# A hand-written order for a recurrent attention and token mixer: every operation re-ordered, other PSUM banks, and 196 more transposed blocks in two 64-row halves

## The chip, the cores and the metric

The program runs on one core of a Trainium2 chip. A core has a matrix engine (PE, whose weight loads the profile lists apart as PEld), a vector engine (DVE), an activation engine (ACT), a general engine (POOL) and a queue that issues transfers (SP). Each engine runs its own list of instructions strictly in order and waits at an instruction until the semaphores that it needs have been raised. Matmuls write to PSUM, which has 8 banks of 512 float32 per partition; all other data are in SBUF.

The metric is device time in microseconds (us), as the median of three runs: 199.9 us before the change (199.68 to 200.76).

## The reference

Two stages, for batch B = 4, H = 8 heads, S = 768 tokens, D = 40. The first is a recurrence over the tokens, with a 40 x 40 state for each batch and head. The second mixes the output over tokens and channels.

```python
for t in range(S):
    y[t]  = r[t] @ state                                   # per batch and head
    Sa    = state @ a[t]
    state = state * w[t] - outer(Sa, b[t]) + outer(v[t], k[t])
x = y as (B, S, 320)
theta  = x @ w_theta
zr, zi = x * cos(theta), x * sin(theta)
u      = x + w_tok_r @ zr + w_tok_i @ zi                   # over the tokens
out    = u + relu(u @ w_ch)
```

## The kernel before

The recurrence is done in chunks of 128 tokens: 6 chunks for each batch, 24 in all, numbered i = 0 to 23. For a chunk the kernel loads w, k, b, a, v and r (160 KB each, in rows of 160 bytes) and does the following.

- `prep(i)`: ln w on ACT, running sums as matmuls (`cs`, `cx`), exponentials on ACT (`exp`, `ew`), products that scale k, b and a (`kb`, two of them, and `ah`, mostly on POOL, line 456), and casts of v and r. Then the scaled k and b (`tkb`, 8 blocks), a (`ta`, 4), v (`tv`, or `to` and `tb` in chunks 0 to 7) and r (`tr`, 8) are transposed in blocks of 128 x 128 on PE. Copies on ACT or DVE bring the result from PSUM to SBUF (`ekb`, `ea`, ...).
- `attention_scores(i)` and `readout(i)`: four 128 x 128 score matrices per head (`spsi`, `sphi`, `slv`, `slu`, line 603). They are matmuls over 64 rows. Each is masked as it leaves PSUM (`mpsi`, `mphi`, `mlv`, `mlu`): on DVE in one multiply (line 612), or on ACT with a second pass on POOL (lines 614 and 616).
- `recurrence(i)`: the serial part. `x0` needs the state of the chunk before, then come `nx`, `nu`, `enu`, the new state (`gt`, `egt`, `wgt`) and its transpose (`gd`, `egd`).
- `y` and `ex` give x for the chunk. `theta(i)` transposes x (`xt`) and multiplies by w_theta (`th`). `sines` takes cos and sin on ACT, and `z` multiplies them with x, on POOL (line 894) or on DVE (line 893).
- `mix_row`: for each of the 24 output blocks, 12 matmuls over the tokens (`row`, line 910), a sum on DVE (`uadd`, line 916), a transpose (`ut`), the channel matmul (`ch`), and the result (`oo`) and its store. They need all z of their batch, so the rows of one batch run among the chunks of the next, and those of the last batch at the end.
- The mixer's weights: `wdma` issues 18 transfers on POOL's queue (lines 961 and 989): w_theta and w_ch in 6 pieces of 160 or 40 KB, and 12 blocks of rows of the two token matrices at 192 KB each. `wt` transposes the token matrices on PE.

Nothing is scheduled at run time. The kernel records 1602 operations, and `order()` then emits them by three tables. `ORDER` is one list over all operations; an engine gets its own operations in the sequence in which they stand there. `HOMES` gives each PSUM tile its bank. `PICK` names operations that take their other form: a copy on the other engine, a mask on ACT and POOL instead of DVE, a product on the other engine, or a transpose in halves.

```python
def order(self):
    for n, m in PICK.items():
        o = self.ops[n]
        o.eng, o.fn = o.alts[m - 1][:2]
        if o.eng == "PE":
            o.new = (o.new[0], 2)          # a transpose in halves takes two banks
    out = [self.ops[n] for n in ORDER]
```

A transpose has two forms (`turned`, lines 404 and 408; `turn_runs`, lines 569 and 572 for r and the early v). The whole form is one matmul per block: 128 rows against a 128 x 128 identity. The form in halves is two matmuls per block, rows 0 to 63 and rows 64 to 127, each against a 64 x 64 identity, with the results in two neighbouring banks.

Loads go through SP's queue in the sequence of `ORDER`. Each raw buffer has 2 to 5 copies, so a load waits until the product that read that buffer before is done, and every load behind it waits too. 11 transposes are done by the transfer engines (`CROSSBAR`), the same 11 in both kernels.

## Time and profile before

| what | value |
|---|---|
| timed runs | 199.9 us median, 199.68 to 200.76 |
| profiled execution, first to last instruction | 195.9 us; no other time is given for that execution, so 4.0 us of the median lie outside its span |
| instructions in it | 8473, 3516 of them matmuls |
| PE, DVE, ACT, POOL busy | 184.3, 163.3, 150.6, 145.1 us |
| read from memory, written | 29.54 MB, 3.93 MB |
| granted clock of PE | 0.997 on average |

A row of the page's fifth part names line, engine, operation, output and inputs, then the count, busy time, mean duration in ns, and the idle time ahead of it with what ended that. In the timeline, neighbours of one kind are merged: start, length, engine, line, operation and count. Matmuls overlap, so what one costs PE is read from the distance between starts and not from its length.

### The profile page before, as it was taken

What the parts mean: (1) busy time and instruction counts of PE and PEld (TensorE: products, weight loads), DVE (VectorE), ACT (ScalarE), POOL (GpSimd) and SP (SyncE); (2) the same over time, 40 slices, a digit from 0 to 9 for tenths busy, and PEclk for the clock granted to TensorE, in tenths of its full rate; (3) what the DMA queues carried; (4) which work ended last, traced back from release to release, by engine and by line L of the source; (5) the groups of instructions that cost most, each with busy time, mean ns of one, the idle gap of its engine ahead of it and who ended that gap; (6) DMA issues with size and microseconds to landing.
All of it is one profiled execution on the core that took longest, in us unless ns stands there. A gap on an engine that the chain in (4) does not pass through costs nothing.

```text
span 195.9 us, 8473 instructions
## 1 busy us (share of the span) xinstructions
PE 184.3 (94%) x3516; PEld 145.4 (74%) x3516; DVE 163.3 (83%) x260; ACT 150.6 (77%) x336; POOL 145.1 (74%) x211
## 2 busy tenths in 40 slices
PE   7889899999997999999899999999999999999992
PEld 6767687887786778887577787887788768767661
DVE  5378799999998999898897999999999938664453
ACT  3575879799997997999689599979999867575111
POOL 8367466579969999696699959868879997469100
PEclk9999999999999999999999999999999999999998
DMA  5999897999999999979999997789899977535055
GB/s 118 217 205 182 148 214 157 174 171 206 216 183 166 197 180 185 225 122 200 179 183 158 166 200 129 164 147 180 161 178 203 168 172 102 128 136 74 32 197 172
DMA packets 134646, 32.78 MB, mean 167 GB/s; under 512 B 124816, under 2 KB 134608, under 8 KB 134608
## 3 DMA queue, kind: packets, MB, share of 16 engines
q1 hardware_dynamic: 131680, 29.19, 76.6%
q0 software_dynamic: 2784, 2.97, 9.3%
q8 instruction: 27, 0.44, 0.9%
q10 hardware_dynamic: 144, 0.08, 0.1%
q14 instruction: 11, 0.09, 0.1%
HBM read 29.54 MB, written 3.93 MB: 171 GB/s over the span
## 4 chain that ended last, share of the span: by engine, by line
PE 61%; DMA 12%; POOL 9%; ACT 6%; DVE 4%; SPq 4%; issue 2%; ACTq 0%; DVEq 0%; POOLq 0%
PE banks L910 16%; PE banks L603 9%; PE banks L404 8%; PE banks L792 5%; DMA raw_a<-in_a_dram 4%; DMA raw_kb<-in_k_dram 4%; SPq L436 3%; PE banks L408 3%; DMA uT<-up 2%; PE banks L569 2%; PE banks L663 2%; POOL kb L456 2%; PE banks L686 2%; PE banks L802 2%; DMA raw_v<-in_v_dram 2%
## 5 line engine op out<-in xcount | busy, mean ns | idle before, releaser
L456 POOL TENSOR_TENSOR kb<-raw_kb,ex 128x320 bf16<-128x320 f32 x46 | 37.1, 814 | 8.0 <-DMA raw_kb<-in_k_dram 3.0
L910 PE MATMUL banks<-zr,wtok_r 128*128 128x320 bf16 x144 | 41.0, 300 | 0.2
L910 PE MATMUL banks<-zi,wtok_i 128*128 128x320 bf16 x144 | 40.8, 299 | 0.1
L456 POOL TENSOR_TENSOR ah<-raw_a,we 128x320 bf16<-128x320 f32 x22 | 19.0, 865 | 12.9 <-ACT we L506 4.7
L612 DVE TENSOR_TENSOR lamu<-banks,mask_p 128x1024 bf16<-128x1024 f32 x22 | 26.8, 1219 | 1.5 <-PE banks L603 0.8
L612 DVE TENSOR_TENSOR psi<-banks,mask_p 128x1024 bf16<-128x1024 f32 x22 | 26.8, 1219 | 0.8 <-PE banks L603 0.7
L612 DVE TENSOR_TENSOR phi<-banks,mask_n 128x1024 bf16<-128x1024 f32 x18 | 21.9, 1216 | 1.6 <-POOL r L462 1.3
L612 DVE TENSOR_TENSOR lamv<-banks,mask_p 128x1024 bf16<-128x1024 f32 x17 | 20.7, 1219 | 1.6 <-PE banks L603 1.0
L894 POOL TENSOR_TENSOR zi<-cs,xp 128x320 bf16<-128x320 f32 x22 | 17.2, 791 | 2.0 <-ACT cs L879 1.2
L910 PEld LDWEIGHTS <-wtok_r 128*128 128x128 bf16 x144 | 14.0, 97 | 5.6 <-issue 0.3
L603 PE MATMUL banks<-aT,kbT 64*128 64x128 bf16 x384 | 17.2, 217 | 0.9 <-DVE kbT L426 0.3
L894 POOL TENSOR_TENSOR zr<-cs,xp 128x320 bf16<-128x320 f32 x22 | 17.4, 802 | 0.1
L910 PEld LDWEIGHTS <-wtok_i 128*128 128x128 bf16 x144 | 14.0, 98 | 3.8 <-issue 0.3
L829 PE MATMUL banks<-kb,lamv 128*128 128x40 bf16 x192 | 14.9, 180 | 0.0
L831 PE MATMUL banks<-kb,lamu 128*128 128x40 bf16 x192 | 14.8, 179 | 0.0
L603 PEld LDWEIGHTS <-kbT 64*128 64x128 bf16 x384 | 11.8, 94 | 3.7 <-ACT kbT L422 1.1
L829 PEld LDWEIGHTS <-lamv 128*128 128x128 bf16 x192 | 13.2, 96 | 0.4
L916 DVE TENSOR_TENSOR up<-banks,xp 128x320 bf16<-128x320 f32 x22 | 10.6, 485 | 3.1 <-PE banks L910 2.9
L831 PEld LDWEIGHTS <-lamu 128*128 128x128 bf16 x192 | 13.0, 96 | 0.0
L472 ACT ACTIVATE lw<-raw_w 128x320 bf16<-128x320 f32 x24 | 11.5, 477 | 1.5 <-DMA raw_w<-in_w_dram 1.3
L496 ACT ACTIVATE ex<-banks 128x328 f32<-128x328 f32 (+1 forms) x24 | 10.8, 450 | 2.2 <-PE banks L491 1.1
L822 PE MATMUL banks<-gd,rT 128*128 128x80 bf16 x80 | 12.2, 197 | 0.0
(202 smaller groups left out, 583.0 us busy)
## 6 DMA issues: line engine op xcount, KB each, us to landing
raw_w<-in_w_dram SPq DMA_DIRECT2D x24, 160.0 KB, 4.3
raw_v<-in_v_dram SPq DMA_DIRECT2D x24, 160.0 KB, 3.7
raw_a<-in_a_dram SPq DMA_DIRECT2D x24, 160.0 KB, 3.9
raw_kb<-in_k_dram SPq DMA_DIRECT2D x24, 160.0 KB, 4.2
raw_kb<-in_b_dram SPq DMA_DIRECT2D x24, 160.0 KB, 4.2
raw_r<-in_r_dram SPq DMA_DIRECT2D x24, 160.0 KB, 3.8
out_dram<-oo SPq DMA_DIRECT2D x9, 160.0 KB, 2.6
wrow_i<-in_moe_w_tok_i_dram POOLq DMA_DIRECT2D x6, 192.0 KB, 5.3
```

Of the source, the lines that this page charges most:

```text
L404: nc.tensor.transpose(out=t[:, m * 128:m * 128 + 128], in_=src, identity=ident)
L456: pool = ("POOL", lambda: nc.gpsimd.tensor_tensor(out=dst, in0=in0, in1=in1, op=ALU.mult))
L472: add("ACT", "ln", i, lambda: nc.scalar.activation(out=paired(lw)[:, :, :, 0:D], in_=paired(raw_w[s4]), func=AF.Ln), 473, [("raw_w", s4)], ...
L496: got = add("ACT", "exp", i, lambda: nc.scalar.activation(out=ex[:, :, 0:D] if no_total else ex.rearrange("p h x -> p (h x)"), in_=sums(ps ...
L603: nc.tensor.matmul(t[:, q, g, :], lhsT=lhs[g][rows(q)], rhs=rhs[g][rows(q)], start=True, stop=True)
L612: add("DVE", kindm, i, lambda: nc.vector.tensor_tensor(out=flat, in0=whole(), in1=mask.to_broadcast([128, 2 * G, 128]), op=ALU.mult), 1217 ...
L822: nc.tensor.matmul(t[:, g * 80:g * 80 + 80], lhsT=by_two(rT)[g], rhs=gd[:, 2 * g:2 * g + 2, :], start=True, stop=False, skip_group_check=True)
L829: nc.tensor.matmul(o, lhsT=lamv[:, p, g, :], rhs=kb[:, 0, h, 0:D], start=first, stop=False, skip_group_check=True)
L831: nc.tensor.matmul(o, lhsT=lamu[:, p, g, :], rhs=kb[:, 1, h, 0:D], start=False, stop=True, skip_group_check=True)
L894: pool = ("POOL", lambda: nc.gpsimd.tensor_tensor(out=dst, in0=in0, in1=in1, op=ALU.mult))
L910: nc.tensor.matmul(acc(), lhsT=wtok[nm][j][:, s], rhs=zs[c][:, s], start=n == 0 and c == 0, stop=n == NT - 1 and c == 1)
L916: add("DVE", "uadd", q, lambda: nc.vector.tensor_tensor(out=u, in0=acc(), in1=x, op=ALU.add), 488, [pk, x_key(q)], [u_key(q)], at="row")
```

## The change

All three tables are new, and so is `WARM`, which only names other banks for its 49 warming matmuls. The computation is the same 1602 operations.

- `ORDER`: another sequence on every engine, loads and weight transfers included.
- `HOMES`: other banks for the PSUM tiles.
- `PICK`: 164 entries in place of 135. Transposes in halves grow by 196 blocks net (`tkb` from 8 chunks to 18, `nut` from 2 to 8, `ut` from 1 to 7, `tr` from 6 to 9, `xt` from 5 to 7, `tv` from 5 to 7, `ta` from 7 to 8, `to` and `tb` from 0 to 2 each). Copies, masks and products change engine too: 7 products `z` are on DVE instead of 2, 4 of the products `kb` instead of 2, and 4 copies `ekb` instead of 7.

```diff
-    0, 7, 3, 6, 1, 20, 2, 21, 8, 23, 24, 4, 27, 32, 9, 30, 22, 33, 31, 25, 5, 34, 26, 12, 28,
+    0, 6, 20, 21, 22, 23, 24, 3, 7, 32, 33, 35, 27, 30, 34, 36, 37, 38, 2, 26, 1, 25, 28, 31, 8,
...
-    25: 1, 31: 1, 37: 1, 39: 1, 40: 1, 48: 1, 49: 1, 75: 1, 80: 1, 85: 1, 86: 1, 115: 1, 118: 1,
+    28: 1, 29: 1, 31: 1, 33: 1, 34: 1, 36: 1, 38: 1, 40: 1, 48: 1, 49: 1, 60: 1, 64: 1, 74: 1,
...
-WARM = {21: (0, 25), 30: (1, 4), 33: (2, 1), 28: (1, 8), 41: (1, 11)}
+WARM = {21: (3, 25), 33: (3, 1), 30: (2, 4), 28: (5, 8), 41: (6, 11)}
```

The new file is two lines longer ahead of the functions, so its line numbers are larger by 2: line 410 of the new kernel is line 408 of the old.

Three places show how the instructions move.

First, POOL at the start of the program, after its last memset. `wth`, `wch` and `wrow` are the mixer's weights; `kb` and `ah` are products, and `r` and `o` casts of r and v. Before:

```order
L334 MEMSET wth 64x320
L456 TENSOR_TENSOR kb_128<-raw_kb_73,ex_174 128x8x40
L462 CAST r_136<-raw_r_80 128x16x40
L616 AFFINE_SELECT phi_200<-phi_200 128x1024
L961 DMA wth<-in_moe_w_theta_dram 64x320
L961 DMA wth<-in_moe_w_theta_dram 128x2x320
L456 TENSOR_TENSOR kb_129<-raw_kb_74,ex_175 128x8x40
```

And now:

```order
L336 MEMSET wth 64x320
L963 DMA wth<-in_moe_w_theta_dram 128x2x320
L963 DMA wch<-in_moe_w_ch_dram 64x320 x2
L963 DMA wth<-in_moe_w_theta_dram 64x320
L963 DMA wch<-in_moe_w_ch_dram 128x2x320
L991 DMA wrow_r_247<-in_moe_w_tok_r_dram 128x768
L991 DMA wrow_i_249<-in_moe_w_tok_i_dram 128x768
L991 DMA wrow_i_248<-in_moe_w_tok_i_dram 128x768
L464 CAST r_136<-raw_r_80 128x16x40
L618 AFFINE_SELECT phi_200<-phi_200 128x1024
L458 TENSOR_TENSOR ah_126<-raw_a_69,we_179 128x8x40
L458 TENSOR_TENSOR kb_129<-raw_kb_74,ex_175 128x8x40
```

Eight weight transfers, 1016 KB, now stand ahead of the cast of r. Before, two of them (200 KB) stood behind the first `kb`, cast and select. The product `kb_128` of chunk 0 has gone to DVE.

Second, DVE at the start, after its memsets. `psi` and `lamv` are masked scores, `aT`, `kbT` and `vT` copies of transposes, and `v` a copy of v turned back. Before:

```order
L455 TENSOR_TENSOR ah_125<-raw_a_68,we_178 128x8x40
L422 COPY aT_184<-banks 128x512
L455 TENSOR_TENSOR kb_128<-raw_kb_73,ex_174 128x8x40
L422 COPY v_132<-banks 128x512
L612 TENSOR_TENSOR psi_198<-banks,mask_p 128x1024
L422 COPY v_133<-banks 128x512
L455 TENSOR_TENSOR ah_126<-raw_a_69,we_179 128x8x40
L455 TENSOR_TENSOR kb_129<-raw_kb_74,ex_175 128x8x40
L612 TENSOR_TENSOR lamv_202<-banks,mask_p 128x1024
```

And now:

```order
L457 TENSOR_TENSOR ah_125<-raw_a_68,we_178 128x8x40
L426 COPY vT_193<-banks 128x512
L457 TENSOR_TENSOR kb_128<-raw_kb_73,ex_174 128x8x40 x2
L424 COPY aT_184<-banks 128x512
L428 COPY kbT_187<-banks 128x2x8x64
L614 TENSOR_TENSOR psi_198<-banks,mask_p 128x1024
L457 TENSOR_TENSOR kb_129<-raw_kb_74,ex_175 128x8x40
L981 CAST wth<-banks 64x320
L981 CAST wth<-banks 128x320
L614 TENSOR_TENSOR lamv_202<-banks,mask_p 128x1024
```

Both products of chunk 0 and its copy of the transposed k and b are on DVE ahead of the first mask, and two copies of w_theta stand between the first mask and the second.

Third, PE at the transpose of k and b of chunk 1 (`kb_129`); `wide` holds the identity. Before:

```order
L603 LDWEIGHTS nuT_196
L603 MATMUL banks<-rT_190,nuT_196 128x128
L404 LDWEIGHTS kb_129
L404 MATMUL banks<-wide,kb_129 128x128
...
L569 LDWEIGHTS o_139
L569 MATMUL banks<-wide,o_139 128x32x4
```

And now:

```order
L406 LDWEIGHTS ah_126
L406 MATMUL banks<-wide,ah_126 128x128
L410 LDWEIGHTS kb_129
L410 MATMUL banks<-wide,kb_129 128x64
...
L715 LDWEIGHTS gt_142
L715 MATMUL banks<-wide,gt_142 128x80
```

Eight matmuls of 128 columns have become sixteen of 64 columns, and they now stand between two groups of 128-row matmuls instead of after a group of 64-row ones.

242 rows, old and new, of tables (HOMES, ORDER, PICK) are left out of this document.

## The prediction

> **What bounds the kernel now.** I read the page's slices first, then busy time by stage, the waits of PE, the chain of waits, and the timeline of POOL's transfers.
>
> ```profile
> PE   7889899999997999999899999999999999999992
> DVE  5378799999998999898897999999999938664453
> DMA  5999897999999999979999997789899977535055
> ```
>
> Three resources run at nine tenths for most of the span: PE to the end, DVE to about 155 us, the transfer engines from 5 us to about 110. So the first question is which of them paces which stage.
>
> ```profile
> 10.00:20.00 10.00, 8.57 (x167) 6.90 (x167) 8.49 (x12) 6.43 (x17) 7.17 (x9) 1.00 1.02 196
> 20.00:60.00 40.00, 37.76 (x774) 30.73 (x771) 37.79 (x47) 35.42 (x88) 28.27 (x38) 1.00 0.96 183
> 60.00:100.00 40.00, 38.83 (x852) 30.70 (x853) 36.79 (x54) 35.58 (x76) 34.75 (x50) 1.00 1.02 179
> 100.00:150.00 50.00, 49.75 (x1112) 39.94 (x1111) 47.53 (x74) 45.03 (x106) 43.02 (x58) 1.00 0.92 171
> 175.00:190.00 15.00, 15.00 (x137) 10.62 (x136) 7.73 (x17) 4.43 (x11) 7.10 (x10) 1.00 0.32 78
> ```
>
> The columns are length, then busy time of PE, weight loads, DVE, ACT and POOL, then granted clock, transfer share and GB/s. From 10 to 100 us the transfers are full (0.96 to 1.02) and DVE is at 92 to 95% from 20 us on. From 100 us PE is hardly idle (49.75 of 50, then 15.00 of 15) at a full clock. So work taken from PE pays surely only late in the program. Early, it pays as far as loads and DVE let the chunks come sooner.
>
> ```profile
> PE banks L408 <- POOL ah L456: 1.2, 2, 0.9
> 48.22 7.07 DMA raw_kb<-in_k_dram
> 86.11 8.33 DMA raw_a<-in_a_dram
> raw_a<-in_a_dram SPq DMA_DIRECT2D x24, 160.0 KB, 3.9
> 45.09 0.60 POOL L989 DMA_DIRECT2D wrow_i<-in_moe_w_tok_i_dram  x1
> 85.67 1.14 POOL L989 DMA_DIRECT2D wrow_i<-in_moe_w_tok_i_dram  x2
> 86.79 1.08 POOL L989 DMA_DIRECT2D wrow_r<-in_moe_w_tok_r_dram  x2
> ```
>
> PE's longest wait is for a product on POOL. The chain of waits has two loads of 7 to 8 us, where the median of such a load of a is 3.9. Both stand among `wrow` transfers of POOL's queue. The one at 86.11 us was issued amid four of them, 768 KB between 85.67 and 87.87 us. Such a group thus makes a load up to 8.33 - 3.9 = 4.4 us later.
>
> **What a half block saves.**
>
> ```profile
> 30.30 0.61 PE L569 MATMUL banks<-wide,o 128*128 128x128 bf16 x8
> 30.74 0.28 PE L404 MATMUL banks<-wide,xp 128*128 128x128 bf16 x2
> 127.59 0.41 PE L408 MATMUL banks<-wide,kb 64*128 64x64 bf16 x16
> 127.93 0.31 PE L910 MATMUL banks<-zr,wtok_r 128*128 128x320 bf16 x1
> 133.43 0.39 PE L404 MATMUL banks<-wide,nu 128*128 128x128 bf16 x4
> 133.75 0.29 PE L408 MATMUL banks<-wide,ah 64*128 64x64 bf16 x8
> 133.88 0.40 PE L408 MATMUL banks<-wide,kb 64*128 64x64 bf16 x16
> 134.11 0.22 PE L603 MATMUL banks<-rT,vT 64*128 64x128 bf16 x2
> 180.44 3.26 PE banks L910 x24
> ```
>
> From start to start, eight whole blocks take 0.44 us, 55 ns each. Sixteen halves, eight blocks, take 0.23 us when 64-row work follows and 0.34 when 128-row work follows. Four whole blocks ahead of 64-row work take 0.32 us, where four at 55 ns make 0.22. So a block in halves costs 28 ns, a saving of 27, and a change between 64-row and 128-row work costs 0.09 to 0.10 us in either direction. The last row gives 0.136 us for a `row` matmul.
>
> The new order halves 196 more blocks, 5.3 to 5.5 us. I counted the changes between the two kinds of matmul in the order of PE's instructions: 156 before, 174 now. The 18 more cost 1.6 us. PE's whole gain is 3.8 us, whatever the rest does.
>
> **Where it falls.** I cut the order at two marks that both kernels have: `x0` of chunk 21, and `y` of chunk 23, the last attention work. In the trace before they stand here, the first with its first matmul, the second with its last:
>
> ```profile
> 156.23 0.20 PE L644 MATMUL banks<-gt,aT 128*128 128x80 bf16 x1
> 176.02 0.18 PE L831 MATMUL banks<-kb,lamu 128*128 128x40 bf16 x1
> ```
>
> *To x0(21).* 162 of the blocks: -4.5 us. 14 of the changes: +1.3. Two more parts of `row`, each of two matmuls at 0.136: +0.5. PE: -2.7 us. DVE also loses work here, by these rows:
>
> ```profile
> L612 DVE TENSOR_TENSOR phi<-banks,mask_n 128x1024 bf16<-128x1024 f32 x18 | 21.9, 1216 | 1.6 <-POOL r L462 1.3
> L422 DVE COPY aT<-banks 128x512 bf16<-128x512 bf16 x5 | 2.1, 418 | 0.7 <-PE banks L404 0.7
> L422 DVE COPY kbT<-banks 128x1024 bf16<-128x1024 bf16 x3 | 2.1, 688 | 0.3 <-ACT gd L718 0.3
> L455 DVE TENSOR_TENSOR kb<-raw_kb,ex 128x320 bf16<-128x320 f32 x2 | 1.7, 870 | 1.1 <-DMA raw_kb<-in_b_dram 1.1
> ```
>
> Two masks fewer (-2.4), three copies `kbT` fewer (-2.1), net four small copies fewer at 0.42 (-1.7), two products `kb` more (+1.7), and the rest, one to three short operations of each kind (`ewo`, `ewt`, `eth`, `enu`, `ext`, `ah`), nets to +1.0. Sum: -3.5 us. ACT gains about 1.7 us and POOL 1.9 to this mark. Both were at 90% or less, so I cost that at nothing. If ACT had no room left, it would be its 1.7 us. As PE and DVE both fall, I take the smaller of the two: **-2.7**, with 0 (the loads pace the chunks) and -3.5 as bounds.
>
> *From x0(21) to y(23).* 12 blocks (-0.3), one part of `row` (-0.3), two `ch` and their 64-row pair (-0.7), and one `xt` (-0.2) fewer: **-1.4**. PE is the only full engine here, so I take it in full; the bounds are -1.4 and 0.
>
> *After y(23).* Those two `ch` come back (+0.7), one part of `row` fewer (-0.3), 22 blocks in halves (-0.6), the moved `xt` and two changes (+0.3): **+0.1** for PE. But three of the last eight products `z` of chunk 21 go to DVE, while POOL does the others.
>
> ```profile
> 178.77 1.11 DVE L893 TENSOR_TENSOR zi<-cs,xs 128x320 bf16<-128x320 f32 x1
> 178.74 0.79 POOL L894 TENSOR_TENSOR zi<-cs,xp 128x320 bf16<-128x320 f32 x1
> 181.09 0.54 DVE L893 TENSOR_TENSOR zr<-cs,xs 128x320 bf16<-128x320 f32 x1 [1.21 <-ACT cs L874]
> ```
>
> The same product took DVE 0.54 us, and 1.11 where POOL began one 0.03 us earlier. Three at 0.57 more are 1.7 us ahead of every later `uadd` and `oo` on DVE. The rows hide part of that: DVE was busy 7.73 us of 15 here. I take **+0.5** between 0 and 1.7. The Trainium skill says why ("SBUF — State Buffer", Who interferes with whom): a DVE `tensor_tensor` with both inputs in SBUF and a GpSimd operation that reads SBUF exclude each other, and the second waits for the first to end. By that rule the three products run in turn with POOL's, and this term would be 1.7 and the sum 1.2 us more. The two rows agree with the rule for one pair.
>
> **The start.** What speaks most against the change is POOL's new first rows.
>
> ```profile
> 5.28 0.36 POOL L334 MEMSET wth<- 64x320 bf16 x1
> 7.46 0.81 POOL L456 TENSOR_TENSOR kb<-raw_kb,ex 128x320 bf16<-128x320 f32 x1 [1.82 <-ACT ex L496]
> 10.69 0.72 POOL L462 CAST r<-raw_r 128x640 bf16<-128x640 f32 x1 [2.43 <-DMA raw_r<-in_r_dram]
> 13.02 1.45 POOL L961 DMA_DIRECT2D wth<-in_moe_w_theta_dram  x2
> 11.18 1.23 DVE L612 TENSOR_TENSOR psi<-banks,mask_p 128x1024 bf16<-128x1024 f32 x1 [0.52 <-PE banks L603]
> 13.34 1.09 DVE L455 TENSOR_TENSOR kb<-raw_kb,ex 128x320 bf16<-128x320 f32 x1
> 15.03 1.23 DVE L612 TENSOR_TENSOR lamv<-banks,mask_p 128x1024 bf16<-128x1024 f32 x1 [0.60 <-PE banks L603]
> ```
>
> POOL was idle from 5.64 to 10.69 us but for one product, so eight issues at about 0.6 to 0.7 us fit: that engine loses nothing. The transfers do not fit, since the transfer engines are full then (1.02). The cast of r waited 2.43 us for its load. From 5.6 us there are 1016 KB of weights where 200 KB came at 13 us: 816 KB more among the loads of chunks 0 and 1, at 4.4 us for 768 KB, so up to 4.7 us later. Late are r of chunk 0 and with it `tr`, `slv` and the first `lamv` on DVE, then `kb` and `ah` of chunk 1. DVE's queue makes it worse: its `kb` of chunk 1 and the two copies of w_theta stand ahead of that first `lamv`. Against it stands what DVE has done by its first mask: a second `kb` and a `kbT` (0.87 + 0.69, that is 1.6 us), and the mask no longer waits for a copy in ACT's queue (0.5 to 0.8). I take 4.7 - 1.6 - 0.8 = **+2.3**, with bounds 0 (nothing waits for these loads) and +4.7. What was moved to the start is missing at 45 to 49 us, where PE's wait of 0.9 comes after such a group (one `wrow` at 45.09, three more behind it): **-0.8**, bounds 0 and -1.2.
>
> The Trainium skill bears on it too ("DMA: Bandwidth & Descriptors", Queues, rings and completion order): each transfer engine takes turns between the queues that have work for it, a packet at a time. By that rule SP's loads would share turns with the weights rather than stand behind them, and all loads in flight would slow at once. The sum would then be the rival of the starved start below. No run here shows the turns themselves.
>
> **Sum.** +2.3 - 2.7 - 1.4 + 0.1 + 0.5 - 0.8 = -2.0 us, so a span of 193.9. The span of 195.9 is one execution and the median of the runs 199.9, 4.0 us around it, which the change doesn't touch. Forecast: **197.9 us**, with 196 to 198.9 as its own range (start +0.4 to +3.3). I call 0.5%, 1.0 us, no change.
>
> **Rivals.**
> - *A start that costs nothing* (11%). The loads of chunk 1 land in time after all. For it: DVE did 8.49 of 10 us from 10 to 20, so the loads were hardly late before. Without the +2.3 and the +0.5 the sum is -4.8: 195.1 us.
> - *The chunks go at the pace of the loads* (20%). For it: shares of 0.96 to 1.02 to 100 us, with the same bytes in both. Then x0(21) comes when it came before, the early saving goes into PE's waits, and a late start is caught up. Left is -1.4 + 0.1 + 0.5 = -0.8: 199.1 us, no change. Against it: from 100 us PE was full while the share was 0.92. That the halves don't give what they promise belongs here: each halved tile holds two banks, 171 such tiles instead of 137 by `HOMES`, and PE would wait for a bank.
> - *A starved start* (24%), slower. The whole 4.7 us reaches DVE's queue, and with DVE over 90% busy to 150 us nothing makes it good. With the early gain of 2.7 that is 4.7 - 2.7 - 1.4 + 0.1 + 0.5 = +1.2, 201.1 us; if PE's early gain doesn't show either, +3.9, 203.8. I put it at 202. It decides once the start costs over 4.5 us with the early gain whole, or over 1.8 without it.
>
> **Chances.** The forecast has 45%. It and the cheap start are faster, 56%; the pace of the loads is no change, 20%; the starved start is slower, 24%. The range of 194 to 202 us leaves out the best of the first rival and the worst of the last.
>
> **What would show it.** PE busy falls by about 4 us from 184.3 and 196 matmuls more stand in it, or the count of blocks is wrong. The first `lamv` on DVE starts at 16 to 18 us instead of 15.03; by 15 the start was free, after 19 it was starved. A wait of POOL or DVE for raw_r, raw_kb or raw_a before 25 us carries the same. x0(21) comes before 156 us, and from y(23) to the end it takes 19.5 to 21 us, as before (176.0 to 195.9). DVE's `z` in the last 20 us take near 1.1 us each. I am wrong if PE shows waits of over 1 us for PSUM copies between 60 and 150 us: the new order then has its own gaps, which I have not priced.

## The result, and the profile after

The changed kernel takes 207.4 us (median of four runs, 206.28 to 208.65), the kernel before 200.3 beside it: a ratio of 1.040, with an interval of 1.033 to 1.047. It is slower by 7 to 8 us, where I forecast 2 us faster. The profiled execution has a span of 205.6 us and a time of 207.29, so 1.7 us lie around a span, not 4.0; the span of 195.9 that I worked from was one of the quicker executions of the kernel before (its times lay between 197.0 and 202.2 later on). In all ratios and means here, executions more than 1.5% over the quickest of their kernel are left out, which leaves two of four for three kernels below (the early weights put back, the clock held up, the old start); the medians that some expectations name still hold them.

The slices of the page after, to set beside those of before:

```profile
PE   7687999989898989999499999999999999999991
DVE  5445789999998889889447988999999987788663
PEclk9755599999999999999957999999999999999999
DMA  6998997989898999999789999988797864842045
```

The clock row is new: before it was 9 up to the last slice. From 8 to 25 us and from 103 to 110 us PE ran at half its clock in this execution. The mean clock of the four executions lay between 0.942 and 0.979, and the time does not follow it: 207.44 us at 0.979, 206.28 at 0.954. PE and DVE show a hole in the slice at 98 to 103 us.

The stretches between marks say where the time went. A mark is the first matmul of `x0` of a chunk, or the last of `y(23)`. The marks used stand up to 0.35 us behind these matmuls (x0(14) starts at 113.17 and 123.45 us, x0(21) of the changed kernel at 166.76), so a difference is good to about 0.3 us. The columns are as in the prediction: length, busy time of PE, weight loads, DVE, ACT and POOL, then clock, transfer share and GB/s. First the kernel before, from the start to x0(1), x0(12), x0(14), x0(21), y(23) and the end:

```profile
0.00:21.60 21.60, 17.30 (x245) 14.38 (x246) 14.35 (x41) 11.89 (x26) 13.25 (x36) 1.00 0.94 183
21.60:90.80 69.20, 67.20 (x1404) 54.80 (x1404) 64.79 (x83) 62.78 (x150) 56.60 (x79) 1.00 0.99 182
90.80:113.50 22.70, 21.77 (x462) 16.08 (x458) 20.33 (x37) 17.73 (x38) 19.29 (x27) 1.00 0.97 174
113.50:156.20 42.70, 42.50 (x973) 34.79 (x970) 41.37 (x61) 40.33 (x92) 35.60 (x48) 1.00 0.92 172
156.20:176.00 19.80, 19.50 (x320) 14.44 (x318) 13.07 (x21) 13.31 (x23) 14.31 (x18) 1.00 0.61 133
176.00:195.90 19.90, 16.07 (x136) 10.95 (x132) 9.44 (x20) 4.52 (x12) 6.10 (x8) 0.96 0.41 117
```

And the same stretches of the changed kernel:

```profile
0.00:25.20 25.20, 20.02 (x260) 15.31 (x261) 13.23 (x42) 11.99 (x25) 16.13 (x41) 0.66 0.96 179
25.20:95.90 70.70, 65.71 (x1507) 53.02 (x1505) 64.74 (x81) 62.13 (x150) 53.65 (x73) 1.00 0.94 173
95.90:123.80 27.90, 24.36 (x476) 18.55 (x474) 20.18 (x37) 19.64 (x41) 20.87 (x28) 0.88 0.91 166
123.80:167.00 43.20, 43.15 (x1014) 34.54 (x1011) 41.55 (x59) 40.69 (x92) 36.50 (x49) 1.00 0.87 168
167.00:184.50 17.50, 17.25 (x307) 12.92 (x304) 13.25 (x21) 10.69 (x21) 10.35 (x12) 1.00 0.61 116
184.50:205.60 21.10, 16.82 (x174) 11.15 (x170) 13.38 (x27) 5.43 (x14) 6.30 (x7) 1.00 0.32 103
```

The difference of 9.7 us between these two executions is +3.6 to x0(1), +1.5 to x0(12), +5.2 from there to x0(14), +0.5 to x0(21), -2.3 to y(23) and +1.2 to the end. So the whole loss lies ahead of x0(14). Behind it the change gains 0.6.

In the waits of the changed kernel (who waited for what: us in all, times, longest), PE waits for products on POOL, and POOL and ACT wait for loads. Before, the longest wait of PE for a product on POOL was 0.9.

```profile
PE banks L406 <- POOL ah L458: 4.2, 3, 3.1
POOL ah L458 <- DMA raw_a<-in_a_dram: 10.9, 4, 5.5
POOL r L464 <- DMA raw_r<-in_r_dram: 8.7, 5, 2.6
ACT lw L474 <- DMA raw_w<-in_w_dram: 5.3, 4, 2.0
```

The longest of them, in the timelines of SP, POOL and PE (start, length, what):

```profile
92.36 3.42 SPq L438 DMA_DIRECT2D raw_a<-in_a_dram  x1
90.44 1.12 POOL L991 DMA_DIRECT2D wrow_i<-in_moe_w_tok_i_dram  x2
101.16 0.86 POOL L458 TENSOR_TENSOR ah<-raw_a,we 128x320 bf16<-128x320 f32 x1 [5.53 <-DMA raw_a<-in_a_dram]
102.08 0.40 PE L406 MATMUL banks<-wide,ah 128*128 128x128 bf16 x4 [3.06 <-POOL ah L458]
```

The load of a of chunk 13 was issued at 92.36 us, behind the last four `wrow` (89.14 to 92.09 us), and landed 8.64 us later. That is the pair that I had quoted from the kernel before (86.11 us and 8.33), but now PE comes to it with nothing left to do and stands for 3.06 us. The chain of waits has the load:

```profile
92.36 8.64 DMA raw_a<-in_a_dram
```

### The profile page after: what moved, and what is told of

Read it like the earlier page. It is cut to its first block, busy times and chain, and to the rows that moved or that the text cites. A ratio compares the mean times of both kernels' runs of the same rounds, so it can differ in the third digit from the quotient of the medians.

```text
span 205.6 us, 8880 instructions
## 1 busy us (share of the span) xinstructions
PE 187.3 (91%) x3712; PEld 145.5 (71%) x3712; DVE 166.3 (81%) x262; ACT 150.6 (73%) x337; POOL 143.8 (70%) x208
## 4 chain that ended last, share of the span: by engine, by line
PE 47%; DMA 21%; SPq 10%; POOL 9%; ACT 6%; issue 3%; DVE 1%; POOLq 1%; ACTq 0%
PE banks L912 13%; DMA raw_a<-in_a_dram 9%; PE banks L605 8%; SPq L438 7%; DMA raw_w<-in_w_dram 6%; PE banks L406 4%; PE banks L794 4%; PE banks L410 4%; POOL zi L896 3%; SPq L450 3%; DMA raw_kb<-in_b_dram 2%; POOL kb L458 2%; POOL zr L896 2%; ACT cs L881 2%; DMA raw_v<-in_v_dram 2%
## 5 line engine op out<-in xcount | busy, mean ns | idle before, releaser
L458 POOL TENSOR_TENSOR kb<-raw_kb,ex 128x320 bf16<-128x320 f32 x44 | 35.1, 808 | 7.2 <-PE banks L406 2.7
L614 DVE TENSOR_TENSOR lamu<-banks,mask_p 128x1024 bf16<-128x1024 f32 x23 | 28.0, 1221 | 1.7 <-PE banks L605 1.4
L458 POOL TENSOR_TENSOR ah<-raw_a,we 128x320 bf16<-128x320 f32 x23 | 19.7, 861 | 13.6 <-DMA raw_a<-in_a_dram 10.9
L614 DVE TENSOR_TENSOR psi<-banks,mask_p 128x1024 bf16<-128x1024 f32 x22 | 26.8, 1219 | 2.1 <-PE banks L605 1.6
L614 DVE TENSOR_TENSOR lamv<-banks,mask_p 128x1024 bf16<-128x1024 f32 x16 | 19.5, 1218 | 1.6 <-PE banks L605 0.6
L605 PE MATMUL banks<-aT,kbT 64*128 64x128 bf16 x384 | 18.6, 228 | 0.4 <-ACT nuT L424 0.2
L896 POOL TENSOR_TENSOR zr<-cs,xp 128x320 bf16<-128x320 f32 x19 | 14.9, 793 | 4.4 <-ACT cs L881 4.4
L896 POOL TENSOR_TENSOR zi<-cs,xp 128x320 bf16<-128x320 f32 x20 | 16.6, 854 | 0.1
L605 PEld LDWEIGHTS <-kbT 64*128 64x128 bf16 x384 | 12.9, 99 | 3.1 <-issue 0.9
L464 POOL CAST r<-raw_r 128x640 bf16<-128x640 f32 x11 | 8.1, 735 | 8.7 <-DMA raw_r<-in_r_dram 8.7
L703 POOL TENSOR_TENSOR gt<-sum,ex 128x320 bf16<-128x320 f32 x13 | 9.6, 736 | 5.1 <-DVE sum L699 5.1
```

Source lines behind the costliest of these rows:

```text
L458: pool = ("POOL", lambda: nc.gpsimd.tensor_tensor(out=dst, in0=in0, in1=in1, op=ALU.mult))
L605: nc.tensor.matmul(t[:, q, g, :], lhsT=lhs[g][rows(q)], rhs=rhs[g][rows(q)], start=True, stop=True)
L614: add("DVE", kindm, i, lambda: nc.vector.tensor_tensor(out=flat, in0=whole(), in1=mask.to_broadcast([128, 2 * G, 128]), op=ALU.mult), 1217 ...
L703: add("POOL", "wgt", i, lambda: nc.gpsimd.tensor_tensor(out=new_state, in0=sum_t, in1=wm.to_broadcast([128, 8, D]), op=ALU.mult), 830, [(" ...
L896: pool = ("POOL", lambda: nc.gpsimd.tensor_tensor(out=dst, in0=in0, in1=in1, op=ALU.mult))
```

## The experiments

Each time is the mean of a kernel's executions, "x1.026" the ratio to the kernel before, run beside it (its mean was 198.8 to 200.0), with its interval. Marks are read from one profiled execution of each kernel. Three kernels have the same first 468 operations (the changed one and the two of its variants in which only loads from chunk 12 on move), and their x0(1) came at 25.2, 23.6 and 24.2 us. So marks that differ by up to 1.7 us show nothing by themselves. Operations in `ORDER` are numbers: 57 and 58 are w_theta, 65 to 68 w_ch, 113, 116, 178 and 181 the first four `wrow`, 673 the load of a of chunk 13.

### The start

**The early weights put back.**

```diff
-    46, 57, 66, 68, 58, 67, 178, 181, 116, 40, 41,
+    46, 57, 58, 40, 41,
...
+    390, 356, 116, 359, 360,
+    378, 502, 181, 501, 504,
+    415, 503, 178, 506, 507,
+    416, 546, 66, 550, 551,
+    228, 65, 67, 68,
```

> The changed kernel, with one part undone: the three larger pieces of wch and three of the first four wrow (816 KB in all) go back from the start to about 45 to 49 us and 60 to 80 us, where the kernel before has them; w_theta stays at the start. Theory L (the weights make the loads of chunks 0 to 2 late, and this is the loss of the start): x0(1) comes at 21.5 to 22.5 us where the changed kernel has it at 25.3, y(0) falls by as much, and the time falls by 3 to 4 us, to 203.4 to 204.4. Theory C (the loss of the start is the halved TensorE clock from 7.7 to 25 us, and that comes from the idle 1.59 us of PE before the blocks of o, which are there with or without the weights): the clock stays at 0.50 up to about 25 us, x0(1) stays within 1 us of 25.3, and the time falls by 1 us at most, 206.4 to 207.4. In both the stall at 99 us can come or go with the hour at which the four last wrow and the load of a meet; I read the start by x0(1) and y(0), apart from the whole time.

Measured: 205.7 us, x1.028 (1.020 to 1.037). x0(1) comes at 21.0 us, so theory L holds for the start, and the clock of 0.84 up to there (0.66 in the changed kernel) speaks against theory C. But the time fell by less than 2 us (two executions, 204.6 and 206.7), and x0(12) comes at 96.8, no sooner than with the late start:

```profile
0.00:21.00 21.00, 16.98 (x262) 13.39 (x263) 13.10 (x42) 11.92 (x26) 12.65 (x35) 0.84 0.93 177
21.00:96.80 75.80, 67.88 (x1502) 54.60 (x1502) 64.66 (x81) 62.70 (x150) 57.06 (x79) 0.95 0.98 177
```

The 816 KB are moved between 44 and 78 us instead, at 177 GB/s worth 4.7 us, and the stretch to x0(12) takes 75.8 us instead of 70.7. The transfers are full at 0.98, so it seems that what was taken from the start comes back there. What this execution did gain is the stall at 99 us: x0(12) to x0(14) takes 24.4 us instead of 27.9.

**The clock held up.**

```diff
-WARM = {21: (3, 25), 33: (3, 1), 30: (2, 4), 28: (5, 8), 41: (6, 11)}
+WARM = {21: (3, 25), 33: (3, 25), 30: (2, 4), 28: (5, 12), 44: (5, 6), 41: (6, 30), 120: (1, 24)}
```

> The changed kernel with 73 more warming matmuls of PE (128 x 128 on a tile of constants, no result is read), in the gaps of the start: 24 before the blocks of o at 5 to 7 us, 4 and 6 more ahead of the first scores, 19 before the casts of r at 12.3 to 14 us, 24 before the sums of chunk 2 at 17.1 to 18.6 us. Loads and weights stay where they are. Theory C (the halved clock is the loss): the clock reads 1.00 from 2 us to 25 us, x0(1) comes at 21.5 to 23 us instead of 25.3, the time falls by 2.5 to 4 us, to 203.4 to 205. Theory L (late loads are the loss; PE would wait for them at any clock): the clock is whole, but PE's waits grow by what its matmuls shrink, x0(1) stays within 1 us of 25.3, the time falls by 1 us at most, 206.4 to 207.4.

Measured: 204.6 us, x1.023 (1.014 to 1.033), with 77 warming matmuls more by the edit, not 73. The clock is whole from start to end. The time is what theory C says, but not by its way: x0(1) comes at 23.7 us, 1.5 sooner, which is no more than that mark moves without any edit, and x0(12) at 95.7, which is where it was. So the halved clock of the start cost nothing that lasted. The 3 us again are found at the stall: x0(12) to x0(14) takes 24.3 us here.

**The early weights alone, in the kernel before.** Operations 57, 66, 68, 58, 67, 178, 181 and 116 go ahead of the cast of r (40):

```diff
-    46, 38, 40, 19,
+    46, 38, 57, 66, 68, 58, 67, 178, 181, 116, 40, 19,
```

> The kernel before with one thing of the change alone: the eight transfers of weights (1016 KB) go to the start of POOL's queue, ahead of the cast of r of chunk 0, in the order of the changed kernel. PE's order, and with it the warming matmuls, stay. Theory W (these transfers are the loss of the start): x0(1) 3 us or more later than 21.6, and 202 to 204. Theory R (the new order of PE, DVE and SP in the start and the halved clock are the loss): the clock stays whole, x0(1) is at most 1.5 us later, and the time is within 1.5 us of before.

Measured: 201.5 us, x1.013 (1.008 to 1.017): 2.5 us, with x0(1) at 26.8, 5.2 us late, x0(12) 4.3 late and x0(14) 3.2. Theory W holds for the cause and is a little high for the whole time, since some 2 to 3 us of the lateness are made good. The clock was not whole, as theory R had said it would be: it fell to 0.87 on average up to x0(1).

**The whole new start before the old rest.** The first 160 operations from the new order, the others in the old sequence:

```diff
     158, 159, 186, 144,
-    235, 164, 165, 237,
+    139, 148, 145, 164,
...
```

> The other splice: the first 160 operations in the new order (to about 27 us, with the 1016 KB of weights at the start and PE's halved clock), all the rest as the kernel before has it. Theory K (a late start is kept to the end, since no engine has the room to catch up): x0(1) at 25 us, 203 to 204.5. Theory G (it is given back: the weights that came early are missing at 45 to 49 and 72 to 80 us, and up to 110 us the loads pace, which have a chunk or two in hand): x0(1) at 25 us too, but x0(14) within 1.5 us of 113.5 and 199.5 to 201.5.

Measured: 202.2 us, x1.016 (1.011 to 1.022). x0(1) comes at 24.2 us, x0(14) at 116.2, 2.7 late. That lies between the theories, a little nearer to K. So the new start costs 2.5 to 3.2 us of the 8, and within the intervals the early weights alone can be all of it.

### The halves, and PE's work

**221 blocks whole again.** 40 of PE's entries leave `PICK`:

```diff
-    28: 1, 33: 1, 36: 1, 38: 1, 77: 1, 106: 1, 140: 1, 164: 1, 192: 1, 194: 1, 221: 1, 242: 1,
...
```

> The changed kernel with 221 of its halved blocks whole again (all that the kernel before does not halve; 25 that only the kernel before halves stay whole too). By my unit costs (27 ns a block, 0.09 us for each of 8 changes between 64-row and 128-row work fewer) PE has 5.5 us more: 3.1 before x0(13), 1.6 from there to x0(21), 0.8 behind it. Theory P (PE's work is what paces the whole program): the time rises by 5 to 5.5 us, to 212.4 to 212.9. Theory L (up to x0(13) loads and stalls pace, and PE's saving there goes into its waits): only the 2.4 us behind x0(13) show, 209.3 to 210.3, and y(12) comes within 1 us of where it comes now. If the halves are worth nothing even late (waits for two-bank tiles eat them): 207 to 208.

Measured: 204.3 us, x1.022 (1.015 to 1.029). With 5.5 us more for PE it is 3 us quicker than the changed kernel. Its stretches from x0(1) to x0(12), to x0(14) and to the end:

```profile
25.20:93.60 68.40, 66.61 (x1388) 54.73 (x1388) 64.69 (x82) 62.29 (x150) 53.32 (x73) 1.00 0.99 181
93.60:118.20 24.60, 22.33 (x467) 17.10 (x465) 19.67 (x37) 19.58 (x41) 20.89 (x28) 1.00 0.98 180
118.20:201.20 83.00, 78.94 (x1422) 60.02 (x1418) 68.68 (x105) 56.87 (x124) 52.85 (x67) 1.00 0.69 138
```

PE is idle for 1.8 us between x0(1) and x0(12), where the changed kernel has 5.0 (70.70 less 65.71), and x0(14) comes 5.6 us sooner, without the stall (24.6 us from x0(12)). Only behind x0(14) do the whole blocks cost something: 83.0 us to the end instead of 81.8. All three theories had the time at 207 us or more and missed it, since none had the stall going away. For the halves ahead of x0(14) theory L holds: they are worth nothing. That halves lose by their second bank what they save would look the same. The changed kernel's waits of PE between 21.5 and 113 us speak against it: 0.4 us for a mask that empties a bank, 7.0 for products and casts on POOL.

**3 us more for PE in the kernel before.**

```diff
-WARM = {21: (0, 25), 30: (1, 4), 33: (2, 1), 28: (1, 8), 41: (1, 11)}
+WARM = {21: (0, 25), 30: (1, 4), 33: (2, 1), 28: (1, 8), 41: (1, 11), 271: (0, 6), 327: (0, 6), 387: (0, 6), 524: (3, 6), 572: (4, 6), 626: (0, 6), 675: (2, 6), 729: (2, 6), 778: (1, 6)}
```

> The kernel before with 54 matmuls more on PE whose result is not read, 128 x 128, 3.0 us at 55 ns each, six ahead of x0 of each of the chunks 3 to 11 (32 to 80 us). Theory P (PE's work paces the program there; my sum took its 2.7 us in full): 2.5 to 3.0 us slower than before. Theory L (loads pace, PE waits anyway): 1 us slower at most, and PE's waits between 30 and 112 us shrink by 2 us or more.

Measured: 202.1 us, x1.015 (1.009 to 1.022), that is 3.3 us. x0(12) comes 3.2 us late. Theory P, then, in the old order: more work for PE between 32 and 80 us costs what it weighs. The kernel with whole blocks does not contradict it. In the old order PE is idle for 2.0 us on the way from x0(1) to x0(12) (69.20 less 67.20), so 3 us more don't fit; in the new order it is idle for 5.0. No run takes work from PE in the old order.

### The order of the loads

**One load earlier.** The load of a of chunk 13 goes ahead of eight others:

```diff
-    672, 723, 673, 704, 707,
+    672, 723, 704, 707,
...
-    416, 546, 550, 551,
+    416, 546, 673, 550, 551,
```

> The changed kernel with one load moved: a of chunk 13, which SP issues at 92.4 us as the ninth of nine loads since its tile came free, goes ahead of eight of them (k, two parts of r, b, v, b again, k of chunks 12 to 14), to about 87 us. Nothing else moves. Theory O (SP's order makes it late; the product ah of chunk 13 on POOL waits 5.5 us for it at 101 us, and with it the whole chip stands for 3 us and then runs at half a clock for 4): that wait is under 1 us, PE's wait of 3.0 us at 99 us is gone, the clock stays whole at 104 us, and the time falls by 4 to 6 us, to 201.4 to 203.4. Theory B (the bytes decide: 768 KB of wrow issued from 89.1 to 92.1 us and the loads are one stream, and whichever comes last stops the chunk): the wait goes over to another load (b or k of chunk 13, r of 12), PE still stands for 2 us or more between 92 and 104 us, and the time falls by 1.5 us at most.

Measured: 204.5 us, x1.024 (1.017 to 1.032). PE's wait of 3.06 us at 99 us and the second drop of the clock are gone. The gain is about 3 us, short of theory O's 4 to 6: the next wait is for the casts of v on POOL (2.6 us for raw_v), and x0(12) to x0(14) still takes 25.1 us where before has 22.7:

```profile
93.20:118.30 25.10, 21.97 (x467) 16.59 (x466) 19.64 (x36) 19.49 (x41) 20.44 (x28) 1.00 0.92 167
```

But with the early weights put back, the warmed clock and the whole blocks the stall is not there either, with this load where it was: the longest wait of PE for `ah` from 92 us to 122 is 0.2, 1.4 and 1.3 us. I take it that a small shift in time is enough to miss the four `wrow`. This stretch of the four kernels also shows what the stall was made of. PE is idle for 2.3 to 3.1 us in it, and for 3.5 in the changed kernel; its busy time is 21.6 to 22.3 us instead of 24.4. So of the 2.8 to 3.6 us that are gained, 2.0 to 2.8 are busy time, which goes with the half clock behind the stand, and the smaller part is the standing itself.

**The old start, the new rest.** The first 140 operations from the old order, the weights as in the first experiment:

```diff
     160, 93, 165, 191,
-    140, 136, 161, 166,
+    63, 64, 136, 92,
...
```

> The two orders spliced: the first 140 operations as the kernel before has them (to about 21 us, chunk 1's first products), all the rest in the new order with its banks and halves; wch and three of the first four wrow where the kernel before has them. Theory S (the whole loss is the start, and the stall at 99 us only follows from it): start as before, PE 3.3 us less work behind it, so no slower than before: 196.5 to 199.5. Theory M (the new order from chunk 2 to chunk 13 loses by itself, since its loads and releases follow one another later; PE's saving there goes into waits): x0(1) near 21.6 us as before, but x0(14) 4 us or more later than the 113.5 of before, and 202 to 204 in all.

Measured: 204.4 us, x1.027 (1.019 to 1.035), x0(1) at 21.4 and x0(14) at 119.0. Theory S falls and M holds: with the start of before, the new order still loses 5.5 us on the way to x0(14), at a whole clock and without the stall at 99 us.

```profile
21.40:94.10 72.70, 66.12 (x1481) 52.33 (x1480) 63.42 (x79) 63.18 (x151) 56.16 (x79) 1.00 0.99 178
94.10:119.00 24.90, 21.71 (x468) 16.64 (x467) 19.71 (x37) 19.36 (x41) 20.63 (x28) 1.00 0.96 178
```

From x0(1) to x0(12) PE has 1.1 us less to do than before, DVE 1.4 us less, and both stretches are longer. The transfers are as full as before.

**The same with the one load early, and with the halves ahead of x0(14) whole or kept.** Whole (19 entries of `PICK` fewer), then kept:

```diff
-    140: 1, 192: 1, 194: 1, 221: 1, 242: 1, 286: 1, 307: 1, 357: 1, 362: 1, 370: 1, 441: 1, 504: 1,
...
```

> The spliced kernel with the start of before (140 operations) and the new order behind it, the weights where before has them, the load of a of chunk 13 ahead of the eight others, and the 118 added half blocks that lie before x0(14) whole again: PE has 3.3 us more to do there than with them. Theory L (loads and the products on POOL that wait for them pace up to 112 us; what PE saves there goes into its waits): no slower than the same kernel with these halves, within 1 us of it or faster, and x0(14) at 114 to 116 us. Theory P (PE's work paces there too): 2.5 to 3.3 us slower than with them.

> The same kernel with those halves kept: start of before, weights where before has them, the load of a of chunk 13 early. Against the one spliced at the same place without the early load (206.3 us) it tells what the place of this one load is worth without a late start: theory O (that load is a loss by itself) 2 us or more faster, 202 to 204; theory B (the stream of loads is the limit, whichever comes last) within 1.5 us of 206.3.

Measured side by side: whole 203.8 us, x1.024 (1.018 to 1.030), kept 205.0, x1.030 (1.022 to 1.037). 3.3 us more for PE ahead of x0(14) cost nothing, as theory L says. The early load gains nothing against the x1.027 without it, so theory B holds here: that load was the place where the lateness came out, not its cause.

**SP's whole queue exchanged.** By the two orders, I counted the KB that SP loads or stores up to the last load that a chunk needs (w, a, k and b). The new order has this much more than the old:

| chunk | 10 | 11 | 12 | 13 | 14 | 15 | 16 | 17 |
|---|---|---|---|---|---|---|---|---|
| KB more | -160 | 0 | 0 | 320 | 640 | 320 | 1120 | 1120 |

From chunk 13 on loads for chunks 15 to 18 stand ahead of those that are needed next. Here are SP's places 76 to 93 (the first is 0), by tensor and chunk, old and new:

```diff
-a12 b13 r12 v12 k13 v13 r12 a13 v14 k14 b14 w14 w15 a14 r14 w16 r14 k15
+b12 w14 k13 r12 b14 v12 r12 b13 k14 a13 r14 v14 b16 w16 w15 r14 v13 a14
```

The new queue in the kernel before, the old queue in the changed kernel, and the old queue behind the old start:

> The kernel before with SP's queue alone in the new order. Theory Q: nothing up to chunk 12, then x0(14) at 116.5 to 119 us instead of 113.5, 202.5 to 206 in all. Theory N: within 1.5 us of before.

> The changed kernel with one engine's order undone: SP's queue (all loads of r, k, v, w, a, b, the stores and the transposes it issues) in the order of the kernel before; every other engine, the banks, the halves and the early weights as in the change. By the two orders, the last load that a chunk needs has 0 to 160 KB more or less ahead of it up to chunk 12, but 320, 640, 320, 1120 and 1120 KB more in the changed kernel for chunks 13 to 17, since loads of later chunks stand ahead. Theory Q (this is the loss between chunk 1 and chunk 14; 640 KB at the 178 GB/s of that stage are 3.6 us, 1120 KB 6.3): the late start stays, x0(14) comes at 116.5 to 119 us, 201 to 203.5 in all. Theory N (the order of the loads is not it; PE, DVE, ACT and POOL lose it among themselves): 205.5 to 208, x0(14) at 120 or later.

> The spliced kernel with the start of before and the weights where before has them (206.3 us, x0(14) at 119.0), and SP's queue in the order of before as well; the new order of PE, DVE, ACT and POOL from chunk 2 on and all halves stay. Theory Q: x0(14) at 113 to 115.5 us, and from there to the end what the changed kernel takes, 81.8 us: 197.5 to 199.5 in all, a little faster than before or the same. Theory N: 204 to 207.

Measured: 205.9 us, x1.035 (1.029 to 1.041), for the new queue in the kernel before. The old queue in the changed kernel gives 213.5, x1.072 (1.066 to 1.079), and behind the old start 213.1, x1.070 (1.063 to 1.077). The first agrees with theory Q in size; the other two go the wrong way under both theories. The wait of ACT for a load of w shows where, in the changed kernel with the old queue:

```profile
ACT lw L474 <- DMA raw_w<-in_w_dram: 12.0, 3, 7.8
```

ACT's new order wants a `w` sooner than the old queue brings it, and PE stood 6.8 us behind that. So a queue and its users have to fit, and the exchange of a whole queue does not tell whether the new pair fits worse. The 205.9 us are no clean proof either: 4.2 us were lost by x0(8), where the counts of KB hardly differ.

**The loads by need.** 47 loads (SP's places 76 to 124) in the order in which their first users stand in the same kernel: in the changed kernel, behind the old start, and as a control in the kernel before. Of the changed kernel's queue, places 76 to 93:

```diff
-b12 w14 k13 r12 b14 v12 r12 b13 k14 a13 r14 v14 b16 w16 w15 r14 v13 a14
+b12 w14 v12 r12 r12 a13 b13 v14 k13 r14 r14 v13 w15 b14 a14 k14 b15 w17
```

> The changed kernel with 47 of SP's loads (its places 76 to 124, chunks 12 to 21) in the order in which their first users stand in the program, each no earlier than its tile comes free there; all other queues, and SP's stores and transposes, stay where they are. Unlike the swap of whole queues, which set SP's order against users from another order and cost 6 us more, this fits the new order. Theory Q (loads that stand ahead of others that are needed sooner cost the new order its time at chunks 13 and 14): x0(12) to x0(14) takes 22 to 24 us instead of 27.9, and 202 to 204 in all. Theory N (no order of the loads helps; the new order of the other engines loses the time): 24.3 us or more there, as in the five other kernels with the new order, and 205 to 208.

> The same order of the 47 loads in the spliced kernel that has the start of before and the weights where before has them (206.3 us, x0(12) to x0(14) 24.9 us). Theory Q: 22 to 23.5 us there, 202 to 204 in all, and the rest over before (2 to 4 us) lies ahead of x0(12). Theory N: 24.3 us or more, 205 to 207.

> The control: the kernel before with the same rule for its loads at places 76 to 124 (33 of 49 change place, most by one to four). Theory Q: they stand nearly in the order of need already, so within 1 us of before, 198.5 to 200.5, perhaps up to 1 us faster. If it loses 2 us or more, the order of need is not what a good order of loads is, and Q falls as it stands.

Measured: 205.6 us, x1.031 (1.025 to 1.037), then 204.0, x1.022 (1.016 to 1.029), and the control 198.8, x0.999 (0.994 to 1.003), the same as before.

```profile
96.30:120.20 23.90, 21.80 (x467) 16.60 (x466) 21.86 (x36) 19.23 (x41) 21.47 (x29) 1.00 0.92 173
94.70:118.80 24.10, 21.98 (x474) 16.83 (x472) 22.28 (x37) 19.65 (x41) 21.67 (x29) 1.00 0.93 173
91.40:112.90 21.50, 21.05 (x451) 15.64 (x448) 19.76 (x36) 17.32 (x37) 19.51 (x27) 1.00 0.99 175
```

These are x0(12) to x0(14) in the three. In the changed kernel it takes 23.9 us instead of 27.9, and the time falls by 1.8 us, which the end of the stall explains; behind the old start it takes 24.1 instead of 24.9, and the ratio goes from 1.027 to 1.022, within the intervals. That is short of theory Q both times. By the marks the order of these loads bears about 1 us; by the times it can't be told from nothing.

### The late part alone

**New from 112 us on, and from 158 us on.** The first 975 or 1320 operations from the old order, the rest in the new:

```diff
     980, 997, 1011, 982,
-    1001, 998, 981, 1002,
+    470, 1133, 1266, 1112,
...
```

> The two orders spliced late: the first 975 operations as the kernel before has them (to about 112 us, all the transfers of weights and the loads up to chunk 18 among them), the rest in the new order with its banks, halves and products on DVE. By my unit costs PE has 1.4 us less work behind x0(14). If PE paces that part (it was busy 49.75 of 50 us there), and the end gives back 0.5 to 1.0 us as in the changed kernel (y(23) to the end 21.3 us instead of 20.3): 0.5 to 1.0 us faster than before, about 199. The rival, that the new late part gains nothing (its waits for two-bank tiles and its products on DVE take the 1.4 us): within 0.4 us of before.

> The kernel before up to its operation 1320 (about 158 us, behind x0(21) and the last loads), and the new order, banks, halves and products z from there on. My sum gave -1.4 to y(23), +0.1 and +0.5 behind it: 0.8 us faster than before. By the trace of the changed kernel, where x0(21) to the end takes 38.6 us instead of 39.4, it is the same 0.8. The rival: the seam and the products z on DVE take it all, within 0.4 us of before or slower.

Measured: 205.0 us, x1.030 (1.024 to 1.037), and 199.6, x1.004 (0.998 to 1.010). The first is inconclusive for the question put. In its profiled execution, the longest of the six (207.8 us), PE stood for 3.5 us at 131 us behind POOL, where the new order has the cast of v of a chunk ahead of its products and the old queue brings that v late:

```profile
133.46 0.45 POOL L463 CAST v<-raw_v 128x320 bf16<-128x320 f32 x1 [4.62 <-DMA raw_v<-in_v_dram]
```

That looks like a wait of the seam. The second gave no gain, where my sum has 0.8 us; its rival holds. What the late part is worth without a seam can be read from the kernels above behind x0(14): with the new late order x0(14) to the end took 81.6 to 83.8 us (twelve kernels, mean 82.8), with the old one 82.4 to 84.5 (six, mean 83.4).

### What the loss is made of, and what stays open

Of the 8 us, the new start costs 2.5 to 3.2 by itself, in the kernel before. The stall at 99 us, with the half clock behind it, costs about 3, and four edits that have little in common took it away; whether each execution of the changed kernel has it, one profile can't show. But the new order behind the start loses some 5 us by itself (x1.027 and x1.022 with the start of before), so the parts overlap: with the weights back, the way to x0(12) gets longer by what the start gets shorter. As far as intervals of 1 to 2 us can tell, the cause of these 5 us is not the halves, the clock, the stall, or, beyond 1 us, the order of the loads from chunk 12 on.

The transfers are full in both orders, and x0(14) comes when more has been moved. From the start to x0(14), in the kernel before, and with its start and the new order behind it:

```profile
0.00:113.50 113.50, 106.27 (x2103) 85.26 (x2103) 99.47 (x160) 92.41 (x212) 89.13 (x140) 1.00 0.98 181
0.00:119.00 119.00, 105.16 (x2188) 83.29 (x2189) 96.71 (x156) 94.42 (x216) 89.93 (x142) 1.00 0.98 179
```

181 GB/s for 113.5 us are 20.5 MB, 179 for 119.0 are 21.3. The 0.8 MB are 4.4 us. So PE and DVE have less to do there and the transfers more, for chunks that come later. The traces name the loads: when x0(14) starts, SP has issued 107 of its transfers of 160 KB in the kernel before, and 112 in the one with its start, as in the changed kernel. The five are two w, an a, an r and the store of a result. With the loads by need behind the old start they are 110, and 177 GB/s for 118.8 us make 21.0 MB.

That fits loads as the pace, but it does not prove it, since a kernel that is late for another reason has loaded more by then too: with the early weights in the kernel before and its own queue, x0(14) is 3.2 us late, SP has issued 109, and 21.0 MB have come. Left as causes are the first 75 places of SP's queue and the new orders of DVE, ACT and POOL, which hand the load buffers on. I did not separate these. No kernel here beats the kernel before by more than can be measured.

## Why the prediction was wrong, point by point

- **The step that failed** is "as PE and DVE both fall, I take the smaller of the two: -2.7" for the way to x0(21). The work fell, but the time did not: from x0(1) to x0(21) the changed kernel took 7.2 us more (1.5, 5.2 and 0.5). By the order, PE's saving of 2.7 us lies all ahead of x0(14). There the transfers stood at 0.91 to 0.94 too (0.97 to 0.99 before), and the saving went into PE's waits, as the blocks made whole again show. From x0(14) to x0(21), where PE is hardly idle, it had nothing less to do: 42.7 us before, 43.2 after. A cut at x0(14) would have shown it. DVE's part was sized about right: its instructions up to x0(21) add up to 154.2 us before and 150.4 after. But its busy time, which counts neighbours that overlap once, fell only from 140.8 to 139.7.
- **What the sum did not have** is a loss by the new order itself ahead of x0(14), put at nothing. It is some 5 us with the start of before. Its cause stays open.
- **The start** was +2.3, with 4.7 as its bound, and is 3.6 us at x0(1) in the profile (2.0 and 2.6 in the two others with the same start) and 2.5 to 3.2 us in the whole time, where it stands alone. The cause was right (the early weights alone give 2.5) and the sign I had given as possible: the first `lamv` on DVE came at 17.31 us, in the middle of my 16 to 18. Behind it came what I had not priced, the load of a of chunk 1 (POOL waited 4.1 us for it) and that of w of chunk 2 (PE waited 1.1). What the clock cost at x0(1) can't be told from what that mark moves by itself.
- **The relief of -0.8** did not come as time. The wait of 0.9 that I took for it ended at 59.97 us and is gone, but from x0(4) to x0(8) both kernels take 25.9 us; in the new one shorter waits for POOL stand there (0.52, 0.77 and 0.48). The last four `wrow` stayed together, and the load of a among them became the longest stall of the program. I had quoted that pair and put no price on it; I did not ask whether the new order would reach it with work in hand. The wait of the kernel before:

```profile
59.97 0.29 PE L408 MATMUL banks<-wide,ah 64*128 64x64 bf16 x8 [0.91 <-POOL ah L456]
```

- **x0(21) to y(23)**: -1.4 forecast, -2.3 measured. **Behind y(23)**: +0.6 forecast, +1.2 measured, with five products `z` on DVE in 4.3 us, 0.68 to 1.04 each. The sum of the two, -0.8, is close to the -1.1 of the rows and the -0.6 between the means of the kernels behind x0(14), but the late part alone showed no gain (x1.004), so this may be luck. The matmuls are 196 more, as counted; PE is busy for 187.3 us instead of the 180 forecast, since matmuls at half a clock count longer. With the old start, the early load and a whole clock it was 182.7, still 2 to 3 more than forecast; the old start keeps 48 of the blocks whole, which is 1.3 of it, and the rest I did not test.
- **The rivals.** "The chunks go at the pace of the loads" fits the way to x0(14) best, though nothing here proves it; it had 20% and a time of 199.1; "a starved start" had the right sign. The second, in its worst form, had both (a late start and no gain of PE: "+3.9, 203.8"), but I put it at 202 and 24%. The 3.6 us beyond it are the stall and what stayed open; none of my cases held that the new order could lose time of its own ahead of x0(14).
- **"What would show it"** had the row that mattered, waits of POOL and DVE for raw_r and raw_a before 25 us, and they came (2.6 and 4.1 us); but the kernel before had waited 2.4 for raw_r as well, so only the one for raw_a told something. Waits of PE over 1 us between 60 and 150 us came too, but for a product on POOL that waited for a load, not for PSUM copies. x0(21) came at 166.8 us, not before 156, and from y(23) to the end it took 21.1 us, a little over my 21.

## What to carry to other kernels

Cut a forecast where the bound changes, and count what an engine saves only in a stretch where it is the bound by itself. Where PE, DVE and the transfers all stood at nine tenths, 3 us more for PE cost 3.3 us in the old order, and 3.3 us more by whole blocks ahead of x0(14) cost nothing in the new one. When an order by hand changes, give the new order's own waits a term in the sum, and read the queue of loads beside the order of its users. No run here shows that the KB ahead of a load forecast the time. A queue and its users are one order, so they can't be exchanged one by one in an experiment without new waits at the seam. And before reading a cause from a mark, see how far the mark moves between kernels that are the same up to there.

## What the runs showed of the hardware that I had not expected

The granted clock of PE. In the changed kernel it fell to half at 7.9 us, after PE had been busy for 0.35 us of the 2 from 5 to 7 us, and came back only at 25.0, though PE was busy for 15.0 of these 17.1 us and for the last five without a gap. It fell again at 103.5 us, after the 3.06 us in which PE stood at 99 to 102, for 6.9 us.

```profile
5.00:7.00 2.00, 0.35 (x11) 0.13 (x11) 0.49 (x1) 1.07 (x3) 1.94 (x5) 1.00 1.07 204
14.00:20.00 6.00, 4.93 (x56) 3.29 (x57) 2.34 (x4) 2.62 (x8) 1.88 (x3) 0.50 0.92 182
20.00:25.00 5.00, 5.00 (x75) 3.99 (x73) 3.51 (x5) 2.62 (x6) 3.88 (x5) 0.50 1.01 185
```

Matmuls of one form took longer there: `wide,r` x8 1.04 us instead of 0.61. With 25 warming matmuls at 5.13 us PE was busy for 1.77 of the same 2 us and the clock never fell. But the same gap did not always bring the clock down at once. In the kernel with its loads by need, whose start is that of the changed kernel, PE was busy for 0.29 of these 2 us, and the clock stayed whole up to 20 us:

```profile
5.00:7.00 2.00, 0.29 (x3) 0.03 (x4) 0.49 (x1) 1.09 (x3) 1.94 (x5) 1.00 1.09 206
14.00:20.00 6.00, 3.98 (x68) 2.47 (x65) 3.87 (x7) 2.85 (x8) 2.38 (x3) 1.00 0.95 189
20.00:25.00 5.00, 4.64 (x83) 4.07 (x83) 3.08 (x4) 3.44 (x8) 4.11 (x6) 0.66 0.91 170
```

So these runs don't show what lets the clock fall, and one execution is not enough to tell that warming matmuls hold it. The Trainium skill ("TensorE: Matmul & The Clock Gate", What's actually happening) has the clock at half after about 3.4 us of idle PE, and whole again after about 3.4 us of sustained work. The second fall, behind a stand of 3.06 us, is near that, the first came after less idle time, and the return took longer: 5.0 us without a gap at the end of the first fall, and 6.9, of which 6.4 were busy, in the second.
